# An attention, gate and feed-forward kernel on one core: low-half matmuls moved to the end of each sum, and a new order of pieces

## The chip, the cores and the metric

The kernel runs on one core of one Trainium2 chip. The metric is the device time of one execution in microseconds (us), the median of several. The core has five engines that run side by side and wait for each other through semaphores: PE (TensorE, matmul; its weight loads are PEld), ACT (ScalarE), DVE (VectorE), POOL (GpSimd) and SP (SyncE), which issues nearly all transfers.

## The reference

```python
def reference(q, k, v, moe_*, moe2_*):              # cut to what matters
    a = softmax(concat(q k^T / 8 inside a band of +-15 keys, q kmax^T / 8 + log 32))   # kmax: max over 32 keys
    x = a @ concat(v, mean of v over 32 keys)       # (2, 8, 768, 64) -> (2, 768, 512)
    gate = sigmoid(5-tap causal convolution of x)
    g = gate * (x @ w_val)                          # then @ w_out
    h = relu(g @ w_out @ w_in)                      # 512 -> 1024, halves u and v
    s = w_spatial @ layernorm(v) + b_spatial        # 768 x 768 over the sequence
    return (u * s) @ w_out2                         # (2, 768, 512)
```

Some weights arrive as 64-bit floats.

## The kernel before, in words

Every large product is computed to nearly fp32 accuracy from two halves of each operand: a high half (the value cast to a shorter float) and a low half (the rest). A product over a contraction is three matmuls for each chunk of 128: high by high, high by low, low by high. ACT casts the high halves, POOL (sometimes DVE) subtracts to get the low halves, so the low half is always the later one. The helper `mm3` writes these three matmuls next to each other, chunk after chunk.

The program is recorded as pieces, each of some instructions on several engines. Names that the text uses, with an index: `lk`, `lq`, `lv` load k, q and v of a pair of heads (8 pairs, 4 to a batch); `kw` builds the key windows; `score`, `at`, `pv` are scores with softmax, transposes and the product with v for one tick (16 ticks: a pair and a half of the sequence); `put` copies the means of v (`vm`, from `vsum`) into v's tile by a transfer; `gate` is the tanh; `val` is x @ w_val (16 pieces of 12 matmuls of 384 columns); `wp` is w_out @ w_in (8 pieces, the first four being one sweep over four banks; each ends with a matmul by `minus` that takes the scaled high half back out of the bank, and so waits for ACT's scaling); `v` and `u` are the halves of h (12 pieces of 512 columns, 16 of 384); `ws` and `wt` prepare w_spatial; `s` is the product over the sequence (8 plain pieces for the first batch, 14 for the second, which is computed with fewer products); `r` is the result (12 pieces). PSUM has 8 tiles (`psum()`, one bank each), handed out in rotation; `unit()` hands out 28 SBUF buffers in the same way.

`ORDER` is a text of piece names. The position of a piece there is the priority of its instructions. A list scheduler (`Planner.plan`) with a cost for every instruction then decides, engine by engine, which ready instruction goes next, and the program is written out in that order. Engines run their own list strictly in order. An edit of ORDER, or of the order of matmuls inside a piece, therefore shifts instructions on all engines. Every record in the profile carries line 195, where the scheduler issues, so groups are told apart by tiles.

Of the kernel before, what the change touches and what calls it, by code (L numbers as in the profile page):

```python
# [16 lines left out]
P = 128  # L17
# [22 lines left out]
LOOK = {"PE": 0, "ACT": 0, "DVE": 0, "POOL": 100, "SP": 200}  # L40

ORDER = """
    mask*2 wout in1*4 wout cw wp*2 wout masks wout in0*3 lk lq wp*2 lq kw lk kw in0 lv vsum lk*2 score put lq kw score
    wp at wp kw wval vsum score lq score lv*2 pv wp at score at put pv score at score wp lv wval*3 put*2 pv lq pv gate
    val*4 lk*2 ws at*2 score lv kw lv kw score pv*2 v u lq score u*3 at pv at pv gate val*2 vsum val vsum val u*3 put
    v ws*2 v*2 lk v*2 at*2 lq score ws*2 score kw pv*2 u lv ws score*2 lk kw s*4 at lq score*2 s at put*2 s at*2 pv*3
    lv pv at put pv s*2 wt at pv gate val*3 gate val*2 out2 val*3 v*3 out2 v out2 v*2 u*3 wt*2 u s*2 u*3 s out2 u s*5
    r*6 s*2 r*3 s*4 r*3
"""

WIN = 10240 / 3
# [286 lines left out]
def tile_kernel(ctx, tc, q, k, v, vn, w_val, conv_w, w_out, w_in, w_sp, b_sp, w_out2, mask_l, mask_r, eye, out):  # L338
# [328 lines left out]
    def val(i):  # L667
        (b, g), m = divmod(i // KT, NC), i % KT
        need("gate", i // KT + 1)
        need("wval", KT)  # L670
        po = psum()[:, :CH]
        for e in range(KT):
            w = W["val", e, 0]
            mm3(po, [t[:, m * P : (m + 1) * P] for t in w], [X[b, g, e][:, a] for a in (0, 1)], e == 0, e == KT - 1)
        z = Z[b, g][:, m]
        dve.scalar_tensor_tensor(z, z, 1.0, po, op0=ALU.add, op1=ALU.mult)
        gg = G[b, g, m] = gh.get().rearrange("p (a s) -> p a s", a=2)
        copy("ghi", gg[:, 0], z)
        sub("glo", gg[:, 1], z, f(gg[:, 0]))
# [3 lines left out]
    def vhalf(i):  # L683
# [3 lines left out]
        need("wp", KT)  # L687
        po = psum()
        ts_ = slice(t * P - g * CH, (t + 1) * P - g * CH)
        for e in range(KT):  # L690
            mm3(po, [G[b, g, e][:, a, ts_] for a in (0, 1)], W["p", e, 1], e == 0, e == KT - 1)
        if b < B - 1:
            h = hs.get()
        elif t < NT // 2:
# [75 lines left out]
    def fast_s(i):  # L770
# [8 lines left out]
        if first:  # L779
            BANK[key] = psum()[:, :CH]  # L780
        po = BANK[key]
        for t in range(n):
# [9 lines left out]
            for k, (a, c) in enumerate(((0, 0), (0, 1), (1, 0))):  # L792
                pe.matmul(po, A[a], Bs[c], start=first and t == 0 and k == 0, stop=t == n - 1 and k == 2, skip_group_check=True)
# [16 lines left out]
    def uhalf(i):  # L810
        (b, g), m = divmod(i // KT, NC), i % KT
        need("val", KT * (i // KT + 1))
        need("wp", 2 * KT)
        if g == 0:
            U[b, m] = uu.get()
        po = psum()[:, :CH]
        for e in range(KT):
            w = W["p", e, 0]
            mm3(po, [t[:, m * P : (m + 1) * P] for t in w], [G[b, g, e][:, a] for a in (0, 1)], e == 0, e == KT - 1)
# [17 lines left out]
    def spatial(i):  # L837
        if i >= (B - 1) * NC * KT:
            return fast_s(i - (B - 1) * NC * KT)
        (b, g), m = divmod(i // KT, NC), i % KT  # L840
        cs = slice(g * CH, (g + 1) * CH)
        need("v", NT * (b + 1))
        need("u", KT * (i // KT + 1))
        need("ws", NT)
        po = psum()[:, :CH]
        for t in range(NT):
            mm3(po, [w[:, m * P : (m + 1) * P] for w in VN[b, t]], [WS[t][:, a, cs] for a in (0, 1)], t == 0, t == NT - 1)
        finish_s(b, g, m, po, bias[:, cs], str(i))

    os_ = Parts(512, F32)  # L850
# [1 line left out]
    def result(i):  # L852
# [7 lines left out]
        for c in range(parts):  # L860
            cs = slice(c * DM // parts, (c + 1) * DM // parts)
            po = psum()[:, cs]
            for e in range(KT):
                mm3(po, [Y[b, g, e][:, a, ts_] for a in (0, 1)], [w[:, cs] for w in W["out2", e, 0]], e == 0, e == KT - 1)
            act.copy(o[:, cs], po)
            sp.dma_start(out[b, t * P : (t + 1) * P, cs], o[:, cs])

# [14 lines left out]
    def w_product():  # L882
# [17 lines left out]
        for n in (1, 0):  # L900
# [141 lines left out]
```

## Time and profile before

| | |
|---|---|
| median of 3 runs | 287.33 us (287.33 to 287.96) |
| the profiled execution: its own time | 286.44 us |
| its span, first to last instruction | 284.7 us |
| PE busy | 259.7 us, 91% of the span |
| DVE, ACT, POOL busy | 190.0, 166.2, 149.3 us |

Busy time of PE is the time in which at least one matmul is on its way; a matmul's record is longer than the step from one matmul to the next, because they overlap. The time of the profiled execution is 1.7 us more than its span.

### The profile page before, as it was taken

Reading aid. Unit: us, or ns where it says so; the run is one execution under the profiler, and the core shown is the slowest. Engines: PE = TensorE matmul, PEld = TensorE weight load, DVE = VectorE, ACT = ScalarE, POOL = GpSimd, SP = SyncE. Lnnn points to the kernel's source line nnn. Section 1 sums busy time; section 2 is a strip of 40 time slices with the busy share of each in tenths; the row PEclk is TensorE's granted clock in tenths of the full one; section 3 lists DMA queues with packets and bytes.
Section 4 is the critical chain, followed back from the end, with each engine's and each line's share of the span. In section 5 each row is a group of like instructions: output and inputs, shape, how many; then the busy total and the mean of one; then the engine's idle time right before and its main releaser. Section 6 shows DMA issues by size and latency. Waiting matters only on the chain.

```text
span 284.7 us, 5456 instructions
## 1 busy us (share of the span) xinstructions
PE 259.7 (91%) x1958; PEld 228.7 (80%) x1958; DVE 190.0 (67%) x426; ACT 166.2 (58%) x446; POOL 149.3 (52%) x172
## 2 busy tenths in 40 slices
PE   0599987898999999999899997999998999999995
PEld 0367655668889898989889997997898988988985
DVE  2795867698698797465986678973863895741250
ACT  4698965998895835559557891456234561332322
POOL 7689553227764338557544650369556288522050
PEclk9999999999999999999999999999999999999999
DMA  7999995899381144300040007012020330105203
GB/s 197 377 404 273 316 220 137 240 251 336 86 222 59 58 117 146 113 0 3 0 105 1 2 17 198 2 60 89 0 76 1 111 113 0 74 29 194 111 0 111
DMA packets 14330, 34.51 MB, mean 121 GB/s; under 512 B 1949, under 2 KB 4544, under 8 KB 14304
## 3 DMA queue, kind: packets, MB, share of 16 engines
q1 hardware_dynamic: 14112, 34.02, 39.7%
q8 instruction: 15, 0.25, 0.4%
q0 software_dynamic: 192, 0.15, 0.2%
q14 instruction: 11, 0.09, 0.1%
HBM read 29.84 MB, written 3.15 MB: 116 GB/s over the span
## 4 chain that ended last, share of the span: by engine, by line
PE 53%; DMA 21%; ACT 9%; DVE 7%; POOL 5%; issue 2%; SPq 1%; POOLq 0%; DVEq 0%; ACTq 0%
PE ps L195 53%; DMA u<-in_moe_w_in_dram 6%; ACT a L195 5%; DMA u<-in_v_dram 5%; DVE u L195 4%; POOL u L195 4%; ACT u L195 4%; DMA u<-in_moe_w_val_dram 4%; DMA u<-in_moe_w_spatial_dram 3%; DMA u<-vm 3%; SPq L195 1%; DVE ps L195 1%; DVE a L195 1%; POOL a L195 1%; ACT aT L195 0%
## 5 line engine op out<-in xcount | busy, mean ns | idle before, releaser
L195 PE MATMUL ps<-u,u 128*128 128x384 f32 (+3 forms) x1434 | 229.8, 346 | 16.1 <-ACT u L195 12.2
L195 PEld LDWEIGHTS ps<-u,u 128*128 128x128 f32 (+1 forms) x1434 | 201.3, 200 | 38.3 <-ACT u L195 14.0
L195 POOL TENSOR_TENSOR u<-u,u 128x384 fp32r<-128x384 f32 (+3 forms) x76 | 102.5, 1364 | 90.5 <-ACT u L195 80.0
L195 ACT CAST u<-u 128x384 fp32r<-128x384 f32 (+3 forms) x76 | 45.8, 636 | 46.0 <-DVE u L195 34.4
L195 POOL TENSOR_TENSOR a<-a,sm 128x360 f32<-128x360 f32 x32 | 26.3, 844 | 28.4 <-DVE sm L195 17.2
L195 DVE SCALAR_TENSOR_TENSOR u<-ps,cw,u 128x384 f32<-128x384 f32 (+3 forms) x64 | 37.0, 607 | 0.0
L195 ACT ACTIVATE u<-ps 128x512 fp32r<-128x512 f32 (+2 forms) x44 | 23.5, 565 | 20.7 <-PE ps L195 16.6
L195 ACT ACTIVATE a<-ps,nm 128x120 f32<-128x120 f32 x48 | 17.0, 363 | 5.5 <-DVE nm L195 4.5
L195 ACT ACTIVATE a<-a,nm 128x120 f32<-128x120 f32 x48 | 18.5, 394 | 2.8 <-DVE nm L195 1.7
L195 DVE BATCH_NORM_STATS2 st<-u 128x6 f32<-128x512 f32 x12 | 8.3, 693 | 16.4 <-ACT u L195 16.4
L195 DVE TENSOR_SCALAR u<-u 128x512 uint32<-128x512 uint32 (+1 forms) x21 | 13.0, 627 | 7.6 <-DMA u<-in_moe_w_out_dram 5.3
L195 DVE TENSOR_TENSOR u<-u 128x384 f32<-128x384 f32 (+5 forms) x28 | 17.9, 650 | 0.2
L195 ACT ACTIVATE ps<-u 128x512 f32<-128x512 f32 x20 | 12.8, 647 | 6.0 <-DMA u<-in_moe_w_in_dram 3.1
L195 DVE SCALAR_TENSOR_TENSOR u<-ps,u 128x512 uint32<-128x512 uint32 x20 | 13.7, 689 | 2.6 <-ACT ps L195 1.4
L195 PEld LDWEIGHTS ps<-aT,u 120*64 120x64 f32 x384 | 12.5, 137 | 3.5 <-issue 1.7
L195 PE MATMUL ps<-aT,u 120*64 120x64 f32 x384 | 13.8, 225 | 1.6 <-DMA u<-in_v_dram 1.4
L195 ACT COPY aT<-ps 120x384 f32<-120x384 f32 x32 | 13.9, 494 | 1.9 <-PE ps L195 1.8
L195 ACT COPY u<-ps 128x512 f32<-128x512 f32 (+1 forms) x13 | 6.8, 562 | 13.6 <-PE ps L195 13.6
L195 DVE TENSOR_TENSOR u<-ps,u 128x384 fp32r<-128x384 f32 (+1 forms) x20 | 10.9, 552 | 5.0 <-ACT u L195 4.0
L195 DVE TENSOR_SCALAR sm<-ps 128x3 f32<-128x3 f32 x32 | 5.1, 159 | 13.7 <-ACT a L195 13.3
L195 DVE TENSOR_TENSOR u<-u,u 128x384 f32<-128x384 f32 (+2 forms) x16 | 14.0, 889 | 0.1
L195 DVE TENSOR_TENSOR gatef<-ps,u 128x384 f32<-128x384 f32 x6 | 3.3, 557 | 15.2 <-PE ps L195 15.2
(54 smaller groups left out, 197.4 us busy)
## 6 DMA issues: line engine op xcount, KB each, us to landing
u<-in_moe_w_spatial_dram SPq DMA_DIRECT2D x12, 384.0 KB, 3.3
u<-in_moe_w_out_dram SPq DMA_DIRECT2D x8, 512.0 KB, 10.4
u<-in_moe_w_in_dram SPq DMA_DIRECT2D x8, 512.0 KB
ks<-in_k_dram SPq DMA_DIRECT2D x8, 384.0 KB, 8.1
u<-in_q_dram SPq DMA_DIRECT2D x8, 384.0 KB, 9.3
u<-in_v_dram SPq DMA_DIRECT2D x16, 192.0 KB, 9.0
u<-in_vn_dram SPq DMA_DIRECT2D x8, 384.0 KB, 7.5
out_dram<-u SPq DMA_DIRECT2D x11, 256.0 KB, 2.8
```

Source lines behind the costliest of these rows:

```text
L195: getattr(real, method)(*args, **kw)
```

## The change: order inside the sums, and a new ORDER

A new helper `product` takes the list of operand pairs of one sum and writes the matmuls in another order: first, for each chunk, high by high and the product with the low half that is ready early; then, for all chunks, the product with the low half of the operand that comes late. `late` says which of the two operands that is. `val`, `v`, `u`, `s` (both batches) and `r` use it. In the first sweep of `wp` the three kinds go one after the other over the four banks. ORDER is replaced; so the scheduler's lists change on every engine. The numbers of instructions of each kind on each engine are the same in both programs.

```diff
+    def product(o, pairs, late, first=True, **kw):
+        todo = [(a[0], b[0]) for a, b in pairs], [(a[0], b[1]) for a, b in pairs], [(a[1], b[0]) for a, b in pairs]
+        todo = [x for y in zip(todo[0], todo[1] if late == 0 else todo[2]) for x in y] + (todo[2] if late == 0 else todo[1])
+        for i, (a, b) in enumerate(todo):
+            pe.matmul(o, a, b, start=first and i == 0, stop=i == len(todo) - 1, **kw)
...
-        for e in range(KT):
-            mm3(po, [G[b, g, e][:, a, ts_] for a in (0, 1)], W["p", e, 1], e == 0, e == KT - 1)
+        product(po, [([G[b, g, e][:, a, ts_] for a in (0, 1)], W["p", e, 1]) for e in range(KT)], 0)
...
-                for e in range(KT):
-                    mm3(pos[e], [t[:, e * P : (e + 1) * P] for t in W["ot", i, 0]], W["in", i, n], i == 0, i == KT - 1)
+                for k, (a, b) in enumerate(((0, 0), (0, 1), (1, 0))):
+                    for e in range(KT):
+                        pe.matmul(pos[e], W["ot", i, 0][a][:, e * P : (e + 1) * P], W["in", i, n][b], start=i == 0 and k == 0, stop=i == KT - 1 and k == 2)
...
-    mask*2 wout in1*4 wout cw wp*2 wout masks wout in0*3 lk lq wp*2 lq kw lk kw in0 lv vsum lk*2 score put lq kw score
+    wout in1 mask wout mask wp in1 wp in1 wout wp cw in1 wout wval in0*4 wp lk wp kw lq lk kw masks score lq score lq
```

**First place: PE, the first sweep of wp.** Before, at the end of the first chunk (`ps_104` is the fourth bank; `mrow`, `mcol` and `edge` are the attention mask, two tiles of which are built here):

```order
L195 MATMUL ps_103<-u_88,u_85 128x512 x2
L195 MATMUL ps_104<-u_88,u_85 128x512 x3
L195 LDWEIGHTS mcol
L195 MATMUL ps_107<-mrow,mcol 128x360
L195 LDWEIGHTS mcol
L195 MATMUL ps_107<-edge,mcol 64x16
```

Now, at the same place (`ps_92` to `ps_95` are the four banks, `u_98` holds the second chunk of w_in, `u_91` the second of w_out):

```order
L195 MATMUL ps_93<-u_88,u_85 128x512
L195 MATMUL ps_94<-u_88,u_85 128x512
L195 MATMUL ps_95<-u_88,u_85 128x512
L195 MATMUL ps_92<-u_98,u_85 128x512
L195 MATMUL ps_93<-u_98,u_85 128x512
L195 MATMUL ps_94<-u_98,u_85 128x512
L195 MATMUL ps_95<-u_98,u_85 128x512
```

The second chunk now follows the first at once, and the four mask matmuls moved behind all 48 matmuls of the sweep.

**Second place: ACT, the scaling of wp4 and wp5.** Before (`a_148`, `a_149` are the exponentials of tick 1, `ps_150` and `ps_156` the sums of wp4 and wp5, `a_169` tick 2):

```order
L195 ACTIVATE a_149,ps_145<-ps_145,nm_146 128x120
L195 ACTIVATE u_123<-ps_150 128x512
L195 COPY u_157<-ks_78 128x12x64
L195 COPY aT_153<-ps_152 120x384
L195 ACTIVATE u_151<-ps_150 128x512
L195 COPY aT_155<-ps_154 120x384
L195 ACTIVATE ps_160<-u_159 128x512
L195 ACTIVATE u_151<-ps_156 128x512 x2
```

Now (`ps_127` is wp4, `a_140` and `a_141` tick 0, `a_146` and `a_147` tick 1, `ps_158` wp5):

```order
L195 ACTIVATE u_128<-ps_127 128x512
L195 CAST u_112<-u_149 128x512
L195 ACTIVATE a_140,ps_136<-ps_136,nm_138 128x120 x3
L195 ACTIVATE a_141,ps_137<-ps_137,nm_138 128x120 x3
L195 ACTIVATE a_146,ps_142<-ps_142,nm_144 128x120 x3
L195 ACTIVATE a_147,ps_143<-ps_143,nm_144 128x120 x3
L195 ACTIVATE u_128<-ps_158 128x512 x2
L195 ACTIVATE a_166,ps_162<-ps_162,nm_164 128x120 x3
```

The scaling of wp4 moved ahead of the exponentials of ticks 0 and 1, that of wp5 behind all twelve of them.

**Third place: POOL, the clearing of v's last tile** (after which SP may issue the loads of the last pair; `u_442` before, `u_389` now). Before, with the softmax scaling of tick 15 (`a_416`, `a_417`) ahead of it:

```order
L195 TENSOR_TENSOR u_419<-u_278,u_419 128x384
L195 TENSOR_TENSOR a_416<-a_416,sm_415 128x360
L195 TENSOR_TENSOR a_417<-a_417,sm_415 128x360
L195 TENSOR_TENSOR u_419<-u_278,u_419 128x384
L195 MEMSET u_442 32x2x64 x2
```

Now, with tick 13 (`a_376`, `a_377`) ahead of it and tick 14 (`a_409`) behind:

```order
L195 TENSOR_TENSOR a_376<-a_376,sm_375 128x360
L195 TENSOR_TENSOR u_365<-u_348,u_352 128x512
L195 TENSOR_TENSOR a_377<-a_377,sm_375 128x360
L195 MEMSET u_389 32x2x64 x2
L195 TENSOR_TENSOR va_396<-va_396,power 128x1
L195 TENSOR_TENSOR u_386<-u_385,u_386 128x768
L195 TENSOR_TENSOR u_390<-u_385,u_390 128x768
L195 TENSOR_TENSOR a_409<-a_409,sm_408 128x360
```

The clearing now stands two ticks earlier, ahead of the last two low halves of w_spatial (`u_386`, `u_390`).

## Rows read from the trace of the kernel before

**Rows 1.** Page, part 1: busy time and share of the span, instructions.

```profile
span 284.7 us, 5456 instructions
PE 259.7 (91%) x1958; PEld 228.7 (80%) x1958; DVE 190.0 (67%) x426; ACT 166.2 (58%) x446; POOL 149.3 (52%) x172
```

**Rows 2.** Busy time by stretch, with granted clock, DMA share and GB/s.

```profile
core 0: us, PE busy (x) PEld busy (x) DVE busy (x) ACT busy (x) POOL busy (x), PEclk, DMA share, GB/s
0.00:20.00 20.00, 9.35 (x28) 6.32 (x29) 12.69 (x19) 12.67 (x23) 14.16 (x29) 1.00 0.91 321
20.00:40.00 20.00, 18.44 (x130) 13.32 (x128) 14.65 (x29) 18.00 (x49) 15.38 (x23) 1.00 1.04 287
40.00:60.00 20.00, 16.42 (x210) 12.41 (x211) 14.04 (x36) 14.47 (x57) 5.09 (x8) 1.00 0.83 196
60.00:80.00 20.00, 18.68 (x220) 16.57 (x218) 16.31 (x38) 17.36 (x51) 13.86 (x20) 1.00 0.80 228
80.00:110.00 30.00, 29.55 (x224) 27.09 (x219) 25.60 (x63) 21.07 (x66) 12.43 (x14) 1.00 0.43 125
110.00:200.00 90.00, 86.65 (x745) 80.05 (x744) 62.49 (x157) 54.29 (x156) 51.26 (x56) 1.00 0.16 48
```

**Rows 3.** Groups by form, PE: busy, mean ns of one, idle before.

```profile
L195 PE MATMUL ps<-u,u 128*128 128x384 f32 x654 | 120.5, 338 | 2.1 <-ACT u L195 1.3 <-POOL u L195 0.6 <-ACT aT L195 0.2
L195 PE MATMUL ps<-u,u 128*128 128x512 f32 x372 | 93.7, 403 | 11.6 <-ACT u L195 10.9 <-POOL u L195 0.4 <-ACT aT L195 0.3
```

**Rows 4.** Timeline, PE, 0 to 26 us: start, length, what, idle before.

```profile
10.34 5.81 PE L195 MATMUL ps<-u,u 128*128 128x512 f32 x12 [10.34 <-ACT u L195]
15.95 0.52 PE L195 MATMUL ps<-mrow,mcol 67*128 67x360 bf16 x1
...
16.83 0.20 PE L195 MATMUL ps<-edge,mcol 67*64 67x16 bf16 x1
17.34 8.46 PE L195 MATMUL ps<-u,u 128*128 128x512 f32 x36 [0.31 <-ACT u L195]
```

**Rows 5.** Timeline, PE, 186 to 192 us.

```profile
185.81 5.36 PE L195 MATMUL ps<-u,u 128*128 128x384 f32 x30
191.45 4.91 PE L195 MATMUL ps<-u,u 128*128 128x512 f32 x19 [0.27 <-ACT u L195]
```

**Rows 6.** What PE waited for, 20 to 110 us: total, times, longest.

```profile
PE ps L195 <- ACT u L195: 4.0, 5, 1.4
PE ps L195 <- DMA u<-in_q_dram: 1.6, 1, 1.6
```

**Rows 7.** Timeline, PE, 36 to 67 us, around its waits, and 78 us.

```profile
36.36 0.50 PE L195 MATMUL ps<-u,minus 128*128 128x512 f32 x1 [0.52 <-ACT u L195]
...
40.11 0.50 PE L195 MATMUL ps<-u,minus 128*128 128x512 f32 x1 [0.77 <-ACT u L195]
...
51.95 0.51 PE L195 MATMUL ps<-u,minus 128*128 128x512 f32 x1 [1.40 <-ACT u L195]
...
66.56 0.50 PE L195 MATMUL ps<-u,minus 128*128 128x512 f32 x1 [0.85 <-ACT u L195]
...
78.58 1.62 PE L195 MATMUL ps<-aT,u 120*64 120x64 f32 x48
```

**Rows 8.** Timeline, ACT, 42 to 50 us and 76 to 79 us.

```profile
42.88 0.36 ACT L195 ACTIVATE a<-ps,nm 128x120 f32<-128x120 f32 x1 [1.43 <-DVE nm L195]
...
43.33 0.36 ACT L195 ACTIVATE a<-ps,nm 128x120 f32<-128x120 f32 x1
...
48.67 0.36 ACT L195 ACTIVATE a<-ps,nm 128x120 f32<-128x120 f32 x1 [2.87 <-DVE nm L195]
...
76.82 0.85 ACT L195 COPY aT<-ps 120x384 f32<-120x384 f32 x2
```

**Rows 9.** Groups by form, ACT.

```profile
L195 ACT CAST u<-u 128x384 fp32r<-128x384 f32 x32 | 14.8, 512 | 14.0 <-DVE u L195 7.9 <-POOL u L195 4.8 <-PE ps L195 1.3
L195 ACT CAST u<-u 128x768 fp32r<-128x768 f32 x12 | 10.0, 836 | 14.7 <-DVE u L195 11.1 <-DMA u<-in_moe_w_spatial_dram 2.1 <-POOL u L195 1.4
L195 ACT COPY u<-ks 128x768 f32<-128x768 f32 x8 | 6.6, 841 | 3.1 <-POOL u L195 3.1
```

**Rows 10.** Timeline, PE, 126 to 221 us, around its waits.

```profile
126.11 1.89 PE L195 MATMUL ps<-u,u 64*64 64x120 f32 x48
127.93 1.62 PE L195 MATMUL ps<-aT,u 120*64 120x64 f32 x48
...
137.65 5.53 PE L195 MATMUL ps<-u,u 64*64 64x120 f32 x66 [0.79 <-POOL u L195]
143.77 2.55 PE L195 MATMUL ps<-u,u 128*128 128x384 f32 x13 [0.60 <-POOL u L195]
...
169.53 0.82 PE L195 MATMUL ps<-ident,a 128*120 128x128 f32 x6
170.59 3.24 PE L195 MATMUL ps<-u,u 128*128 128x384 f32 x17 [0.24 <-ACT aT L195]
175.27 1.99 PE L195 MATMUL ps<-aT,u 120*64 120x64 f32 x48 [1.44 <-DMA u<-in_v_dram]
...
220.68 3.59 PE L195 MATMUL ps<-u,u 128*128 128x384 f32 x19 [0.84 <-ACT u L195]
```

**Rows 11.** Chain that ended last, 168 to 221 us: start, length, what.

```profile
168.29 0.20 POOL u L195
...
171.11 4.02 DMA u<-in_v_dram
...
175.27 1.87 PE ps L195 x46
...
215.72 1.28 ACT u L195
...
217.07 2.95 POOL u L195
...
220.03 0.61 ACT u L195
...
220.68 3.42 PE ps L195 x18
```

More of the change, by code (lines that the diff above doesn't have):

```diff
@@ L42 @@
 ORDER = """
-    mask*2 wout in1*4 wout cw wp*2 wout masks wout in0*3 lk lq wp*2 lq kw lk kw in0 lv vsum lk*2 score put lq kw score
[L44 to L48, printed above, removed]
+    wout in1 mask wout mask wp in1 wp in1 wout wp cw in1 wout wval in0*4 wp lk wp kw lq lk kw masks score lq score lq
+    wval lk vsum lv lk kw wp vsum score lk lq put wp kw score lv put score at pv wval lv at pv lk wp score put wval at
+    pv lv put ws*3 at score pv vsum gate val*3 kw val score at*2 pv*2 v u*2 vsum at lq at pv kw pv gate u score*2 val
+    u ws lv lk kw lk kw val*3 lq score*2 v lq put lv put v at v at*2 v score*2 pv lv pv ws u*2 lv ws u*2 v at*2 put lq
+    score*2 out2 pv*3 s*4 at*2 s*2 at pv put pv*2 s*2 gate val*3 gate val*2 out2 val*3 out2 v out2 v u v*4 u*3 wt*3 r
+    s*3 u s u*3 s*2 r*3 s*6 r*2 s r*2 s r*4
 """
@@ L671, in val @@
         po = psum()[:, :CH]
-        for e in range(KT):
-            w = W["val", e, 0]
-            mm3(po, [t[:, m * P : (m + 1) * P] for t in w], [X[b, g, e][:, a] for a in (0, 1)], e == 0, e == KT - 1)
+        product(po, [([t[:, m * P : (m + 1) * P] for t in W["val", e, 0]], [X[b, g, e][:, a] for a in (0, 1)]) for e in range(KT)], 1)
         z = Z[b, g][:, m]
@@ L781, in fast_s @@
         po = BANK[key]
+        pairs = []
         for t in range(n):
@@ L791, in fast_s @@
                 Bs = [y[:, k_ * CH : (k_ + 1) * CH] for y in FT[t]]
-            for k, (a, c) in enumerate(((0, 0), (0, 1), (1, 0))):
-                pe.matmul(po, A[a], Bs[c], start=first and t == 0 and k == 0, stop=t == n - 1 and k == 2, skip_group_check=True)
+            pairs.append((A, Bs))
+        product(po, pairs, 0, first, skip_group_check=True)
         if x == 1:
@@ L816, in uhalf @@
         po = psum()[:, :CH]
-        for e in range(KT):
-            w = W["p", e, 0]
-            mm3(po, [t[:, m * P : (m + 1) * P] for t in w], [G[b, g, e][:, a] for a in (0, 1)], e == 0, e == KT - 1)
+        product(po, [([t[:, m * P : (m + 1) * P] for t in W["p", e, 0]], [G[b, g, e][:, a] for a in (0, 1)]) for e in range(KT)], 1)
         o = U[b, m][:, g * CH : (g + 1) * CH]
@@ L845, in spatial @@
         po = psum()[:, :CH]
-        for t in range(NT):
-            mm3(po, [w[:, m * P : (m + 1) * P] for w in VN[b, t]], [WS[t][:, a, cs] for a in (0, 1)], t == 0, t == NT - 1)
+        product(po, [([w[:, m * P : (m + 1) * P] for w in VN[b, t]], [WS[t][:, a, cs] for a in (0, 1)]) for t in range(NT)], 0)
         finish_s(b, g, m, po, bias[:, cs], str(i))
@@ L862, in result @@
             po = psum()[:, cs]
-            for e in range(KT):
-                mm3(po, [Y[b, g, e][:, a, ts_] for a in (0, 1)], [w[:, cs] for w in W["out2", e, 0]], e == 0, e == KT - 1)
+            product(po, [([Y[b, g, e][:, a, ts_] for a in (0, 1)], [w[:, cs] for w in W["out2", e, 0]]) for e in range(KT)], 0)
             act.copy(o[:, cs], po)
@@ L914, in w_product @@
                 need(f"in{n}", i + 1)
-                for e in range(KT):
-                    mm3(pos[e], [t[:, e * P : (e + 1) * P] for t in W["ot", i, 0]], W["in", i, n], i == 0, i == KT - 1)
+                for k, (a, b) in enumerate(((0, 0), (0, 1), (1, 0))):
+                    for e in range(KT):
+                        pe.matmul(pos[e], W["ot", i, 0][a][:, e * P : (e + 1) * P], W["in", i, n][b], start=i == 0 and k == 0, stop=i == KT - 1 and k == 2)
                 if i == KT - 1:
```

## The prediction

> **What bounds the kernel now.** I began with the busy times and then asked where the busiest engine stands still. PE is busy for 259.7 of 284.7 us, DVE for 190.0, ACT for 166.2 [rows 1]: the kernel is bound by PE, and 25.0 us of the span are without a matmul. Neither program has a matmul more or less than the other, so the change can move only PE's standstill, and its slow start. The reader is to look at two things: the steps of a dense stretch, and the places between.
>
> In a dense stretch thirty matmuls of 384 columns take 5.36 us [rows 5]; less one record of 0.338 us [rows 3] that is 5.02 over 29 steps, 0.173 us a step. For 512 columns 36 take 8.46 us [rows 4]; less a record of 0.403 [rows 3], 8.06 over 35 steps is 0.230. These hold whatever follows whatever: a weight load goes with every matmul (1958 of each [rows 1]), also where two matmuls in a row use the same weights. Writing high by high, low by high in turn therefore costs nothing by itself. Since a record is 0.165 us longer than a step, a stop costs some 0.165 us more than the idle time that a row names.
>
> The stretches say where the stops are [rows 2]. PE's idle time is 10.65 us up to 20 us (10.34 of it ahead of the first matmul [rows 4]), then 1.56, 3.58 and 1.32 in three stretches of 20, then 0.45, and 3.35 in the 90 us from 110 on. From 20 to 80 us ACT is the next engine, busy 49.83 of 60, with DMA at 0.80 to 1.04 and the loads far behind their issue. The list of waits gives the names [rows 6]: five waits of PE for ACT, 4.0 us, one of 1.6 for q. Four of the five are the matmul by `minus` at the end of a wp piece [rows 7]: PE stands behind ACT's scaling of that bank. After 110 us the waits are single and of several kinds [rows 10].
>
> **The change part by part.** I sum against the profiled execution (span 284.7 us, its own time 286.44) and apply the difference to the median 287.33; its time is 0.89 below the median, which is the error of that step.
>
> *A, the sweep of wp.* The first load, its casts and so the first matmul are in the same order on SP, DVE and ACT, so the start stays at 10.34. Before, twelve matmuls go at (5.81 - 0.40)/11 = 0.49 us a step, four mask matmuls follow, PE stops for 0.31, and 36 go at 0.230 until 25.80 [rows 4]. The first pace is about that of the lower of the clock's two levels, 1.2 GHz, the second of 2.4; the row of granted clock says 1.00 for the whole stretch and does not resolve it [rows 2]. Somewhere between 15.95 and 17.34 the pace changed; I take 16.7. Now 13 matmuls fit before that, and 35 at 0.230 plus the end of a record bring 24.9, so -0.9. The w_out chunk that is needed last is the eighth load in both orders. The masks come back later at the fast pace: 1.08 us of slow records [rows 4], half of it, +0.5. A is -0.4, between -0.9 and 0.
>
> *B, from the sweep to the transposes of tick 5.* This is ACT's stretch. The transposes' copies end at 77.7 [rows 8] and pv4 starts at 78.58 [rows 7]. Up to the same copies ACT now has four casts of 384 columns (the high halves of val0 to val3) and two of 768 (ws1, ws2) more, and one copy of 768 less: 4 x 0.512 + 2 x 0.836 - 0.841 = 2.9 us [rows 9]. Against it: PE's wait of 1.6 for q goes, because tick 3 is placed later, and with it some of the 2.87 us in which ACT stood ahead of tick 3's exponentials [rows 8]; I take the smaller, since q of pair 3 is issued later too. And PE has more behind it at pv4: seven matmuls of v0 (7 x 0.230 = 1.6) less one tick of scores, half of 1.89 [rows 10], so 0.65. B is 2.9 - 1.6 - 0.65 = +0.65. Its bounds are far apart. If all six waits of PE go, -(4.0 + 1.6 + 6 x 0.165) = -6.6; if ACT gives nothing back and the waits at wp grow, some +4.5 (the rival below). I stay by the sum of ACT's own work, since ACT has only 10 us to spare in these 60. The work is not wasted: ws1, ws2 are then done, but PE is dense from 80 to 110 anyway, so nothing is taken back there, and I count 0.
>
> *C, 110 us to the products of the second batch.* Five waits stand here: 0.79, 0.60, 0.24, 1.44 [rows 10] and 0.27 [rows 5], 3.34 us, with 5 x 0.165 some 4.2. The 1.44 us is the load of v for the last pair: POOL clears its tile at 168.29, SP issues after that, the transfer lands at 175.13 (171.11 + 4.02) [rows 11]. The clearing now stands on POOL two ticks earlier, ahead of the last w_spatial halves, and pv14 comes behind s5 rather than inside val9; this wait goes. The 0.79 and 0.60 are POOL's: the key windows of tick 12 and the low half of the last w_spatial tile. The windows are built some twenty POOL operations earlier now, and the low halves of v and w_spatial end each sum, as `product` does it, with 26 matmuls of s0 to s2 (4.5 us) ahead of the first use of the last tile. The 0.24 and 0.27 lie in tick 15's wake and go with it. What is late next: v5's high half. ACT casts it behind ten exponentials of ticks 14 and 15, 0.455 us a step [rows 8], 4.6 us, on top of two ticks' copies, two w_spatial casts and three pv's. PE has meanwhile two pairs of transposes (1.6), two ticks of scores (1.9), three pv's (2.4) [rows 10] and those 4.5, 10.4 us. That is about even; I put 0.5 there and 0.7 for what I do not see. C is -4.2 + 1.2 = -3.0, between -4.2 and 0.
>
> *D, the end.* One wait, 0.84 at 220.68 [rows 10]. The chain runs from PE through an ACT cast of 1.28, a POOL subtraction of 2.95 and an ACT operation of 0.61 back to PE [rows 11]: the slow low halves of v hold a buffer, ACT cannot write the next relu, and PE finds no bank. Now u12 is scaled ahead of u10 and u11, and r0 to r2 and six s sums are open meanwhile, so I leave the wait in: 0, between -1.0 and +1.0. The result pieces at the very end are the same 24 matmuls.
>
> The sum is -0.4 + 0.65 - 3.0 + 0 = -2.75: span 282.0, median 284.6.
>
> **The rivals.** *Slower, by ACT at wp5 to wp7.* Between the scalings of wp4 and wp5 ACT now has all twelve exponentials of ticks 0 and 1, 12 x 0.455 = 5.5 us, and these begin some 1.4 us behind PE's scores. PE's own work up to wp5's `minus` matmul is the rest of two ticks (1.2), nine matmuls of wp5 (2.1), tick 2 (0.95 and its masks) and two of wp6 (0.5), about 5.0. So PE stands for 2.5 us where it stood for 0.77 [rows 7], and wp6 and wp7 stand behind six more exponentials and behind two ticks and two pv's in the same way, 1 us each beyond what they were. With ACT's 2.9 not recovered B becomes +4.5, and the time 287.33 - 0.4 + 4.5 - 3.0 = 288.4. For it: four of the five waits for ACT are of just this kind. Against it: wp4 is scaled earlier, wp7 has two ticks of other work around it. It decides from B = +4.3.
>
> *No change.* The work after 110 us could run into banks. Three pv sums (pv10 to pv12) now wait on DVE behind the reading of s0 to s2, so seven sums are open when the transposes of tick 13 ask for two banks. Two convolutions of four steps and their sums cost 3 us there, which makes C 0 and the time 287.6. The trace speaks for such a mechanism with the 0.84 us of D, against it with nothing of the kind between 80 and 200 us. The Trainium skill (PSUM — Partial Sum Buffer, Specifications) gives eight banks per partition, and a sum that is kept open for its late half holds one of them longer: by that rule alone the change lengthens every hold and the time would not fall; the trace agrees only at 220.68, with 0.84 us.
>
> *Faster by more.* The waits for ACT and q before 80 us go as well: B about -3.5, time 280.4. For it: ACT idles 5.5 us from 40 to 60 [rows 2]. Against it: ACT's 2.9 us more.
>
> That the reordered sums do nothing because the low halves were ready anyway is likely for most sums; it would leave ORDER's effect, most of C, standing.
>
> **How the numbers follow.** The forecast with its own range of 283.0 to 285.8: 0.48; faster by more: 0.14; a small gain between: 0.05; no change: 0.16; slower: 0.17. A difference of 0.3%, 0.9 us, is about what a measurement of this kernel can tell from none. So faster is 0.67, same 0.16, slower 0.17. From 280.7 to 288.2 holds all but some 0.06 below and 0.13 above.
>
> **What would show it.** A: the 48 matmuls of the sweep without a stop, ending near 24.9. B: pv4 starting at about 79, and waits of PE for ACT between 20 and 80 of 3 to 5 us. If one of them at wp5 exceeds 2.5, the slower rival is at work. C: no wait for v after 110 us and PE idle there under 1.5 us where it was 3.35. D: a wait of about 0.8 near u12. The prediction is wrong if pv4 starts after 82, if the transfers issued ahead of put0 land late enough to hold pv0, or if a wait of over 2 us shows at s0 or at the transposes of tick 13.

## The result, and the profile after

After: 279.28 us (median of 4 executions, 279.03 to 281.12), before beside it 287.33 (4 executions, 286.47 to 287.96); the ratio is 0.974, 95% interval 0.969 to 0.979. The forecast was 284.6, with a range from 280.7 to 288.2: the kernel became faster by 8 us and not by 2.75, and ended below the range. Medians, here and below, are of all executions of a kernel; the ratios leave out those over 1.5% above the kernel's fastest.

Part 1 of the page of after, as [rows 1]:

```profile
span 277.3 us, 5457 instructions
PE 259.3 (94%) x1958; PEld 229.0 (83%) x1958; DVE 191.1 (69%) x426; ACT 166.2 (60%) x446; POOL 150.8 (54%) x172
```

PE's busy time fell by 0.4 us, its standstill from 25.0 to 18.0. So the frame of the prediction held: only standstill and slow matmuls could go. The stretches of after, as [rows 2], with the last one added:

```profile
core 0: us, PE busy (x) PEld busy (x) DVE busy (x) ACT busy (x) POOL busy (x), PEclk, DMA share, GB/s
0.00:20.00 20.00, 11.04 (x38) 8.33 (x39) 13.04 (x21) 13.11 (x22) 14.87 (x30) 1.00 0.93 342
20.00:40.00 20.00, 16.72 (x131) 11.13 (x129) 14.32 (x30) 17.83 (x50) 13.92 (x19) 1.00 1.04 298
40.00:60.00 20.00, 18.78 (x205) 14.25 (x205) 13.78 (x38) 17.14 (x61) 9.11 (x14) 0.91 0.78 195
60.00:80.00 20.00, 19.76 (x207) 16.87 (x204) 17.20 (x38) 18.06 (x59) 14.32 (x13) 1.00 0.93 254
80.00:110.00 30.00, 29.87 (x282) 27.65 (x280) 25.78 (x65) 22.30 (x71) 14.75 (x22) 1.00 0.25 70
110.00:200.00 90.00, 88.98 (x722) 83.17 (x721) 65.93 (x167) 52.55 (x149) 49.61 (x56) 1.00 0.19 56
200.00:278.00 78.00, 74.14 (x386) 67.57 (x384) 41.05 (x72) 25.20 (x42) 34.22 (x22) 0.99 0.20 71
```

Up to 20 us PE has 38 matmuls behind it where it had 28, and there is a new thing: a granted clock of 0.91 from 40 to 60. The sweep of wp in PE's timeline, as [rows 4], with the stops behind it:

```profile
8.81 13.96 PE L195 MATMUL ps<-u,u 128*128 128x512 f32 x49 [8.81 <-ACT u L195]
22.62 0.33 PE L195 MATMUL ps<-mrow,mcol 67*128 67x360 bf16 x1
...
23.61 0.99 PE L195 MATMUL ps<-u,minus 128*128 128x512 f32 x2 [0.54 <-ACT u L195]
```

The sweep starts 1.53 us earlier and runs without a stop that the timeline names (one gap, ahead of its fifth matmul, is 0.14 us). The row's 49 matmuls, the last of them wp4's, end at 22.77, so the sweep itself ends at 22.55 where it ended at 25.80. What PE waited for, first from 20 to 110 us, as [rows 6], then from 110 us to the end:

```profile
PE ps L195 <- ACT u L195: 3.4, 4, 1.8
PE ps L195 <- DVE u L195: 1.3, 1, 1.3
```

```profile
PE ps L195 <- ACT aT L195: 0.6, 1, 0.6
PE ps L195 <- DVE nm L195: 0.3, 1, 0.3
```

The waits for v and at u12 [rows 10] are gone, and so is the one for q [rows 6]; the one for DVE, 1.3 us ahead of tick 0's scores, is new.

To compare programs with different orders I take, from PE's records, three points at which PE has done the same work in both, to one or two matmuls: the end of val7, the end of val15 and the end of the last matmul. Before: 104.8, 191.2, 281.5. After: 101.6, 185.9, 274.1. So 3.2 us were gained up to val7, 2.1 from there to val15 and 2.1 behind it, together 7.4, which is the difference of the spans.

### The profile page after: what moved, and what is told of

Its sections match the earlier page's. It is cut to its first block, busy times and chain, and to the rows that moved or that the text cites. A ratio compares the mean times of both kernels' runs of the same rounds, so it can differ in the third digit from the quotient of the medians.

```text
span 277.3 us, 5457 instructions
## 1 busy us (share of the span) xinstructions
PE 259.3 (94%) x1958; PEld 229.0 (83%) x1958; DVE 191.1 (69%) x426; ACT 166.2 (60%) x446; POOL 150.8 (54%) x172
## 4 chain that ended last, share of the span: by engine, by line
PE 57%; DVE 15%; ACT 13%; DMA 9%; issue 4%; SPq 1%; DVEq 0%; ACTq 0%
PE ps L195 57%; DVE u L195 9%; ACT a L195 9%; DMA ks<-in_k_dram 4%; DMA u<-in_moe_w_out_dram 3%; ACT u L195 3%; DVE ps L195 2%; DMA u<-in_moe_w_spatial_dram 2%; DVE a L195 1%; DVE st L195 1%; DVE km L195 1%; SPq L195 1%; ACT aT L195 1%; DVE nm L195 0%; DVE va L195 0%
## 5 line engine op out<-in xcount | busy, mean ns | idle before, releaser
L195 PEld LDWEIGHTS ps<-u,u 128*128 128x128 f32 (+1 forms) x1434 | 201.8, 201 | 32.3 <-ACT u L195 10.2
L195 POOL TENSOR_TENSOR u<-u,u 128x384 fp32r<-128x384 f32 (+3 forms) x76 | 102.9, 1369 | 66.9 <-ACT u L195 65.2
L195 ACT CAST u<-u 128x384 fp32r<-128x384 f32 (+3 forms) x76 | 46.5, 636 | 46.9 <-DVE u L195 24.1
L195 POOL TENSOR_TENSOR va<-va,power 128x1 f32<-128x1 f32 x12 | 7.3, 610 | 21.6 <-DVE va L195 21.5
L195 DVE TENSOR_TENSOR u<-u,u 128x256 f32<-128x256 f32 (+2 forms) x16 | 17.1, 1069 | 0.8 <-DMA u<-in_moe_w_spatial_dram 0.6
L195 DVE TENSOR_TENSOR u<-u 128x256 f32<-128x256 f32 (+5 forms) x28 | 13.8, 497 | 0.3
```

The costliest lines, as they stand in the source:

```text
L195: getattr(real, method)(*args, **kw)
```

## The experiments

The table holds all of them, with before and after; the times of before beside them were 287.0 to 288.0. "First" is the start of the first matmul; the other columns are the three stretches between the points above, in the profiled execution.

| kernel | median us | ratio to before, 95% | first | to val7 | val7 to val15 | val15 to end |
|---|---|---|---|---|---|---|
| before | 287.33 | 1 | 10.34 | 104.8 | 86.4 | 90.3 |
| after | 279.28 | 0.974 (0.969 to 0.979) | 8.81 | 101.6 | 84.3 | 88.2 |
| e1 sums and sweep, old ORDER | 304.10 | 1.054 (1.044 to 1.064) | 10.44 | 104.4 | 93.0 | 100.7 |
| e2 new ORDER alone | 281.83 | 0.980 (0.976 to 0.984) | 8.96 | 105.8 | 82.8 | 88.2 |
| e3 before, loads alternate | 282.51 | 0.982 (0.978 to 0.986) | 8.79 | 101.3 | 85.9 | 90.3 |
| e4 after, loads put back | 287.44 | 0.999 (0.997 to 1.001) | 10.43 | 112.1 | 82.5 | 88.3 |
| l, third load w_out | 284.84 | 0.990 (0.986 to 0.993) | 8.81 | 101.8 | 86.2 | 90.3 |
| l, third load w_val | 287.29 | 0.998 (0.996 to 1.001) | 8.82 | 106.7 | 86.1 | 90.2 |
| g1 sweep alone, old ORDER | 285.82 | 0.994 (0.991 to 0.997) | 10.68 | 107.5 | 85.8 | 90.3 |
| g2 sums alone, old ORDER | 302.13 | 1.048 (1.044 to 1.051) | 10.65 | 106.0 | 93.2 | 97.7 |
| p, after with the old sweep | 281.35 | 0.979 (0.975 to 0.982) | 9.02 | 104.8 | 82.5 | 88.3 |
| p, after with the old sums | 278.86 | 0.970 (0.967 to 0.973) | 8.86 | 104.4 | 82.4 | 88.1 |
| c, v cleared earlier | 289.42 | 1.007 (1.004 to 1.010) | 10.00 | 106.6 | 87.4 | 89.4 |
| d, tail of ORDER alone | 301.29 | 1.047 (1.043 to 1.051) | 10.61 | 105.8 | 85.9 | 103.2 |
| d2, u8 ahead of v8 | 288.77 | 1.003 (1.000 to 1.006) | 10.30 | 106.8 | 85.9 | 91.8 |
| c1, wp5 ahead of tick 1 | 282.63 | 0.982 (0.979 to 0.985) | 9.15 | 106.4 | 82.5 | 89.2 |
| c3, wp5 ahead of ticks 0, 1 | 288.03 | 1.002 (0.999 to 1.005) | 9.15 | 111.2 | 82.6 | 89.2 |
| f1, PE's stop filled | 281.06 | 0.977 (0.973 to 0.981) | 8.69 | 102.9 | 84.4 | 89.5 |
| h1, e3 and g1 together | 283.53 | 0.984 (0.978 to 0.991) | 9.03 | 101.3 | 85.8 | 90.3 |
| h2, h1 and ORDER behind val7 | 282.83 | 0.983 (0.978 to 0.988) | 8.68 | 105.2 | 85.3 | 88.1 |

**The two halves of the change.** e1 is before with the new sums and the new sweep; e2 is after with both as they were.

> The new order inside the sums (and in the sweep of wp) with the old ORDER. Theory P (it is the new ORDER that pays, since most low halves were ready anyway): the median stays within 1.5 us of the kernel before, 286 to 288; the first matmul stays at 10.3 us, since the loads go in the old order; PE's waits for POOL after 110 us (0.79 and 0.60 before) shrink. Theory S (the sums pay: they let PE start work that waited for low halves): 283 or less, with fewer stops between 110 and 200 us.

> The new ORDER with the old order inside the sums. Theory P: 280 to 282, first matmul at 8.8 us as in the changed kernel. Theory S: 284 or more, with stops at matmuls that wait for POOL's low halves; the first matmul still at 8.8.

The sums and the sweep do not work by themselves: beside the old ORDER they cost 16 us. ORDER alone gives most of the gain, 6.1 of 8 us. Both stretches behind val7 are as short with ORDER alone (82.8, 88.2) as in after (84.3, 88.2).

**The first loads.** e3 changes only the first line of before's ORDER, e4 only that of after, where the four chunks of w_in stand in a row again:

```diff
e3
-    mask*2 wout in1*4 wout cw wp*2 wout masks wout in0*3
+    mask*2 wout in1 wout in1*2 wout in1 wout cw wp*2 masks in0*3
e4
-    wout in1 mask wout mask wp in1 wp in1 wout wp cw in1 wout wval
+    wout in1*4 mask wout mask wp*2 wout wp cw wout wval
```

> The kernel before with one edit in ORDER: the first eight loads alternate between w_out and w_in instead of four of w_in in a row (the mask tiles' place is the same, ahead of the last part of the sweep). Theory L (the place of the third load sets PE's start, since ACT's cast of the first w_in chunk stands behind the third load's first step): first matmul at 8.8 instead of 10.3 us, clock up some 1.5 to 3 us earlier, sweep's 48 matmuls done near 23 instead of 25.8, and the whole kernel 1 to 3 us faster, as far as the stops behind it do not take it back. Rival N (the early landing was a chance of that execution): first matmul at 10.3 +- 0.3, time as before within 1 us.

> The changed kernel with one edit in ORDER: all four loads of w_in ahead of the second of w_out, as before. Theory L: first matmul back at 10.3 us, clock up later, sweep done near 25, the kernel 1.5 to 3 us slower than the changed one (281 to 282.5). Rival N: first matmul at 8.8 or anywhere, time of the changed kernel (279.3 +- 0.8).

Both went further than expected: e3 gains 5.4 us, e4 loses all 8. The cause of the start stands in ACT's timeline. Before, up to the first matmul at 10.34 (ACTIVATE is the first step of splitting a loaded chunk, CAST the last on ACT):

```profile
6.61 0.63 ACT L195 ACTIVATE ps<-u 128x512 f32<-128x512 f32 x1 [0.57 <-DMA u<-in_moe_w_in_dram]
9.10 0.66 ACT L195 ACTIVATE ps<-u 128x512 f32<-128x512 f32 x1 [1.85 <-DMA u<-in_moe_w_in_dram]
9.67 0.62 ACT L195 CAST u<-u 128x512 fp32r<-128x512 f32 x1
```

After:

```profile
6.10 0.65 ACT L195 ACTIVATE ps<-u 128x512 f32<-128x512 f32 x1
7.57 0.66 ACT L195 ACTIVATE ps<-u 128x512 f32<-128x512 f32 x1 [0.81 <-DMA u<-in_moe_w_out_dram]
8.14 0.62 ACT L195 CAST u<-u 128x512 fp32r<-128x512 f32 x1
```

The cast that the first matmul needs, of the second load, stands on ACT behind the first step for the third load. In before that is a second chunk of w_in, whose step starts at 9.10, in after a second of w_out, at 7.57; both steps start when the chunk has landed. To see what in the order counts, the next two change the third load alone: "wout in1 wout in1*3" and "wout in1 wval in1*3" for "wout in1*4".

> Before, with the second chunk of w_out loaded third instead of sixth (the three w_in chunks behind it keep their order). Theory T (the third load decides when ACT gets to the cast that the first matmul needs; a second chunk of w_out lands sooner than a second of w_in): first matmul at 8.8 to 9.1 instead of 10.3, time 283 to 286 beside 287.3. Rival Q (all loads must alternate): first matmul at 10 or later, time within 1 us of before.

> Before, with the first chunk of w_val loaded third, ahead of the second chunk of w_in. Theory T (the third load is late where it reads the same tensor as the second): first matmul at 8.8 to 9.1 as with w_out third; the sweep's second chunk comes one load later, so the time is 284 to 288. Rival O (only the number of loads ahead counts, or w_out's place): first matmul at 10 or later, 288 to 290.

The chunk of w_val lands at 7.57 too:

```profile
7.57 0.66 ACT L195 ACTIVATE ps<-u 128x512 f32<-128x512 f32 x1 [0.98 <-DMA u<-in_moe_w_val_dram]
8.14 0.62 ACT L195 CAST u<-u 128x512 fp32r<-128x512 f32 x1
...
17.49 9.85 PE L195 MATMUL ps<-u,u 128*128 128x512 f32 x35 [1.63 <-ACT u L195]
```

Over all kernels the first matmul starts at 8.68 to 9.15 in the twelve whose third load is of w_out or w_val, and at 10.00 to 10.68 in the eight in which it is of w_in. The last of the three rows says why the early start alone is worth nothing: with w_val third, the sweep runs out of chunks, PE stands 1.63 us ahead of the second one, and before's time is back. With w_out third 2.6 us are gained, with both tensors nearly in turn 5.4.

The start is thus only a part of what the order of the loads is worth. In e3 the wait for q is gone as well, and PE waits for ACT for 2.1 us from 20 to 110 us instead of 4.0. In e4 the sweep, too, runs out of chunks:

```profile
10.43 4.86 PE L195 MATMUL ps<-u,u 128*128 128x512 f32 x12 [10.43 <-ACT u L195]
17.27 10.04 PE L195 MATMUL ps<-u,u 128*128 128x512 f32 x36 [1.98 <-ACT u L195]
```

It ends at 27.31, 4.8 us later than in after. From there to pv4 e4 takes 59.9 us and after 54.3. PE's idle time in that stretch differs by only 0.6 us (5.3 and 4.7), but e4 has 13.6 us at half clock there, from 58.8 to 62.2 and from 65.6 to 75.8, and after 3.4: the rest of the difference is slow matmuls.

**Sums and sweep apart.** "p" is after with one of the two put back, g1 and g2 are before with one of the two.

> After's ORDER and its sums of val, v, u, s and r, with the old order of matmuls in the first sweep of wp. With both orders old the time was 281.8, with both new 279.3. Theory S (the sweep's order makes the 2.5 us, by when the clock rises and what ACT does first): 281 to 282.5. Theory P (the product sums make it): 278.5 to 280.

> After's ORDER and its new sweep of wp, with the old order of matmuls in the sums of val, v, u, s and r. Theory S: 278.5 to 280. Theory P: 281 to 282.5. If neither half alone gives 2.5 us, what decides is whether a half-clock spell falls into the stretch up to pv5.

> Before, with the new order of matmuls in the first sweep of wp alone (its sums and ORDER). With after's ORDER this edit saved some 2.5 us. Theory S (a sweep that is served high by high first is better wherever it stands): 284.5 to 286 beside 287.3. Theory O (it only fits the new ORDER; here the loads come late and the masks stand inside the sweep): 286.5 to 290.

> Before, with the new order inside the sums of val, v, u, s and r alone (its sweep and ORDER). Sums and sweep together gave 304.1, with stops of 4.1 us inside s0 and 2.8 at pv15. Theory N (each sum now asks for the operand that counts as early three or more steps sooner, and in the old ORDER it is not there yet): 298 to 304, with the stop at s0 above 3 us. Rival W (the 16 us are the sweep's, by half-clock spells behind it): 286 to 290.

The sweep is the half that gains: 0.970 with it against 0.980 without in the new ORDER (p with old sums against e2; the intervals are apart), and 0.994 in the old one. The sums of `product` gain nothing in the new ORDER (0.974 with, 0.970 without, intervals that overlap) and make the whole loss in the old one. Where, PE's timeline of g2 shows at s0:

```profile
131.23 3.29 PE L195 MATMUL ps<-u,u 128*128 128x384 f32 x18
138.45 2.93 PE L195 MATMUL ps<-u,u 128*128 128x384 f32 x8 [3.93 <-DVE u L195]
```

s0 stops after eight matmuls, high by high and high by low of four chunks, because the ninth needs the high half of v4. ACT's timeline of g2 has the cast of that half at 137.78:

```profile
137.78 0.62 ACT L195 CAST u<-u 128x512 fp32r<-128x512 f32 x1
```

In before the same cast stands at 127.39, together with v3's, ahead of s0's first matmul at 131.67. So it is not four matmuls' difference within the sum (the ninth instead of the thirteenth, 0.7 us). ORDER is the same in both, but the planner lays the engines' lists by its own estimates, and with the new sums it puts the last steps of v4's statistics and its normalising on DVE, 132.65 to 137.26 us, behind most of the softmax of ticks 10 and 11; in before they end at 126.88, ahead of it. Why its estimates tip over there was not tried. This stop is 3.93 of g2's 14 us. Others stand at pv15 (2.58), at s9 (2.77) and from 241 to 249 us (0.49, 1.46 and 0.74), and behind the stops at s0 and s9 matmuls of 384 columns go at 0.32 us a step instead of 0.173; these were not followed to their causes. Beside the new ORDER v4's cast is at 130.92, ahead of s0 at 138.55, and nothing waits.

**Term C: the wait for v.** c moves one token of before's ORDER, the last lv, so that POOL clears v's last tile ahead of s4, the scaling of tick 15 and s5:

```diff
-    s at put*2 s at*2 pv*3 lv pv at put pv s*2
+    s at put*2 lv s at*2 pv*4 at put pv s*2
```

> Before, with the lv token of the last pair alone six tokens earlier in ORDER, so that POOL clears v's last tile ahead of s4, the scaling of tick 15 and s5 instead of behind them; SP can issue its load earlier. pv14 and val8 move up on PE with it. Theory V (the 1.6 us stop at pv14 is only this clearing): the stop goes, val7 to val15 takes 84.5 to 85.0 instead of 86.4, time 286.0 to 286.6 beside 287.9. Rival N (PE then stands for what is next in line, the transposes of tick 15 or val8's operand): 86 or more in that stretch and under 0.6 us gained.

PE's timeline of c at the same place as the 1.44 us of before [rows 10]:

```profile
170.49 1.21 PE L195 MATMUL ps<-aT,u 120*64 120x64 f32 x24 [0.58 <-POOL u L195]
...
175.17 0.79 PE L195 MATMUL ps<-u,u 128*128 128x384 f32 x3 [1.05 <-DVE u L195]
176.77 0.92 PE L195 MATMUL ps<-aT,u 120*64 120x64 f32 x24 [0.81 <-DVE u L195]
```

The wait for v is gone, 1.44 us, and three others stand there, 2.44 (one of them was 0.24 before). The stretch is 1.0 longer. The rival of this experiment holds: the load was only the last of several things that came late there.

**Term D: the wait at u12.** d takes before with after's tokens from the last val pieces on. d2 moves one u token ahead of the third v token, so that ACT empties u8's and u9's banks ahead of v10's:

```diff
d
-    out2 val*3 v*3 out2 v out2 v*2 u*3 wt*2 u s*2 u*3 s out2 u s*5 r*6 s*2 r*3 s*4 r*3
+    out2 val*3 out2 v out2 v u v*4 u*3 wt*2 r s*3 u s u*3 s*2 r*3 s*6 r*2 s r*2 s r*4
d2
-    val*3 v*3 out2 v out2 v*2 u*3 wt*2
+    val*3 v*2 u v out2 v out2 v*2 u*2 wt*2
```

> Before, with after's order of tokens from the last val pieces to the end alone (the same counts of pieces; sums as before). Before has PE stops of 0.44 us at v6 and 1.0 us at u12 there, and 90.3 us from the end of val15 to the end of r11; after has neither stop and 88.2. Theory T (the order of these last pieces is what term D missed): 88.0 to 88.7 in that stretch, time 285.5 to 286.5 beside 287.9. Rival R (the stops go because of what stands earlier, such as the second tick's windows or the w_spatial halves): 90 or more in that stretch, time 287.3 to 288.5.

> Before, with one u token moved ahead of the third v token of the second batch, so that ACT empties u8's bank ahead of v8's and u9's ahead of those of v10 and v11, as in after. Theory B (PE's stop of 1.0 us at u12 is for one of these banks): that stop goes, val15 to the end of r11 takes 88.8 to 89.4 instead of 90.3, time 286 to 286.6 beside 287.3. Rival P (POOL's low halves of v, 2.95 us each, set the pace, and the stop moves to s8 or s10): 90 or more in that stretch, time 287 to 288.

d is far off both theories: the tail without what goes ahead of it costs 14 us, with a stop of 3.66 us at u14 and three more for s10, of 0.83 to 1.89 us. It shows that the tail does not stand for itself, and says nothing on the wait. d2 is cleaner:

```profile
217.81 21.06 PE L195 MATMUL ps<-u,u 128*128 128x384 f32 x110
...
244.16 2.01 PE L195 MATMUL ps<-u,u 128*128 128x384 f32 x10 [1.17 <-ACT u L195]
```

PE runs through u12, as meant, and stands 1.17 us for ACT 25 us later. The rival holds: the chain that ended last runs there through 4.28 us of POOL and 0.84 of ACT to that matmul, and the bank was only where it showed.

**ACT at wp5, and the clock.** After has a stop of 1.82 us at wp5's matmul by `minus`, and a half clock behind it:

```profile
40.42 0.57 PE L195 MATMUL ps<-u,minus 128*128 128x512 f32 x1 [1.82 <-ACT u L195]
```

These are the stretches around it (the row of 3.40 us has the granted clock 0.50):

```profile
36.00:40.70 4.70, 2.88 (x33) 1.74 (x33) 3.89 (x14) 4.18 (x21) 1.58 (x2) 1.00 1.03 267
40.70:44.10 3.40, 3.40 (x9) 2.65 (x9) 1.35 (x5) 2.92 (x13) 1.56 (x2) 0.50 1.07 264
44.10:48.00 3.90, 3.89 (x42) 2.55 (x42) 2.90 (x5) 2.12 (x5) 3.00 (x5) 1.00 0.47 125
```

wp6's matmuls stand 0.43 us apart there instead of 0.23. c1 and c3 move wp5 ahead in after's ORDER ("score lq wp score" and "wp score lq score" for "score lq score ... wp"); f1 leaves the order and fills PE's stop with work:

```diff
         for o in self.plan():
             real, method, args, kw = o.call
+            if fill and o.eng == "PE" and o.piece == ("wp", 6):
+                for i in range(fill):
+                    getattr(real, method)(*args, **dict(kw, stop=True))
+                fill = 0
             getattr(real, method)(*args, **kw)
```

> After, with wp5 one token earlier in ORDER, so that ACT scales wp5's bank between the exponentials of tick 0 and tick 1 instead of behind both. In after PE stands 1.98 us at 38.2 for this scaling and the granted clock is 0.5 from 40.7 to 44.1. Theory K (that stop brings the clock down): both go, some 2.0 us of stop and half of 3.4 us of slow matmuls, 1.7, less up to 1.5 that comes back as a wait for tick 1's exponentials: 275.5 to 277.5, no half-clock rows ahead of the last microseconds. Theory W (ACT is the bound there, the wait only moves): the stop shows again ahead of the transposes of tick 0 or 1, val7 ends at 101 to 102 as in after, time 278.5 to 280.

> After, with wp5 two tokens earlier, so that ACT scales wp5's bank ahead of the exponentials of ticks 0 and 1. Theory K: no stop of 1.98 us at 38 and no half clock behind it, 275.5 to 277.5. Theory W: ACT must wait for wp5's sum before any exponential, and a stop of 1.5 to 3 us shows at wp6, at the scores of tick 2 or at the transposes of tick 0; 279 to 282.

> After, with PE kept at work in the 1.98 us in which it stands ahead of wp5's last matmul: the first matmul of wp6, which stands just ahead of the stop, is issued nine times instead of once (each of the extra eight is a sum of its own that the ninth overwrites; the output stays that of after). 8 x 0.227 = 1.8 us. Nothing else moves. Theory K (the stop brings the clock down): no granted clock of 0.5 at 40.7 to 44.1, wp6's matmuls 0.23 us apart instead of 0.43, and 1.5 to 2 us less, 277.0 to 278.0. Rival A (the clock falls for another reason, or ACT sets the pace there anyway): the spell stays, or it goes and PE waits for ACT behind it; 279 to 279.8.

c1 and c3 are slower than after: ACT's work moves, and PE stands for ACT and DVE elsewhere (c3 up to 2.9 us at wp6). In f1 the stop is gone, and wp6 runs at the full clock:

```profile
40.21 2.14 PE L198 MATMUL ps<-u,u 128*128 128x512 f32 x8
42.19 0.62 PE L200 MATMUL ps<-u,u 128*128 128x512 f32 x2
42.78 0.50 PE L200 MATMUL ps<-u,minus 128*128 128x512 f32 x1
43.12 2.45 PE L200 MATMUL ps<-u,u 128*128 128x512 f32 x10
```

But f1 is not faster. Its profiled execution has another half clock, 28.0 to 34.9 us, behind the stop at score0 that after has too. Three of its six executions show a mean clock of 1.000, no half clock anywhere, and took 279.31, 280.05 and 280.33 us; after's four, at 0.992 to 0.994, took 279.03 to 281.12. So that theory falls: filling the stop takes its half clock away, and no time is gained by it. PE then stands for ACT 0.63 us at wp6, where after has no stop, and 0.80 us at wp7, as in after (0.79).

**Do the stages add?** h1 is e3 with g1's sweep, h2 adds after's tokens behind val7, still with the old sums.

> Before with its first eight loads alternating (282.5 alone) and the new order of matmuls in the first sweep of wp (285.8 alone beside 288.0); old sums, old order of pieces. Theory A (the two add): val7 ends at 98 to 100 and the time is 279.5 to 281. Theory M (with the loads in time the sweep has nothing left to gain): val7 at 101 to 102, 282 to 283.5. Behind val7 the stops of before at s1, s2, pv14, v6 and u12 are all still there, 176 us from val7 to the end of r11.

> h1 with after's order of tokens behind val7; still the old sums. Theory Z (the order of pieces behind val7 makes C and D, whatever stands ahead): 172.3 to 173 us from val7 to the end of r11 as in after, 3.5 to 4.2 us under h1, so 276 to 279. Rival G (the order behind val7 needs the v, u and w_spatial work that after has done ahead of it): new stops of 2 us and more at s0 or at the transposes of tick 13, at or above h1.

With the loads in time the sweep has nothing left to gain in the old order (0.984 against e3's 0.982). In h2 the last stretch is after's, 88.1 instead of 90.3, though the old order stood ahead of val7, but from val7 to val15 it takes 85.3 and not 82.4, with new waits:

```profile
142.14 0.91 PE L195 MATMUL ps<-aT,u 120*64 120x64 f32 x22 [1.28 <-ACT aT L195]
...
150.45 1.84 PE L195 MATMUL ps<-u,u 128*128 128x384 f32 x9 [0.76 <-ACT u L195]
```

That order leans on work that after has done before val7. No experiment beats after by more than the measurement can tell.

## Why the prediction was wrong

Set against the prediction's own steps, in the profiled executions, the 7.4 us come so:

| step | booked | measured |
|---|---|---|
| to the sweep's end (A without the masks) | -0.9 | -3.25 (25.80 to 22.55) |
| from there to pv4 (B without its 0.65, and A's masks) | +1.8 | +1.6 (52.8 us to 54.3) |
| pv4 to the end of val7 (B's 0.65) | -0.65 | -1.5 (26.2 to 24.7) |
| val7 to val15 (C without the wait at v6) | -2.6 | -2.1 |
| val15 to the end (C's wait at v6, and D) | -0.4 | -2.1 |

Two terms are set where their work stands: the 0.65 us of matmuls that are done ahead of pv4 shorten the stretch behind it, and the wait at v6 [rows 5], 0.27 us and 0.165 for the stop, which C took in, lies behind val15.

**A failed, and with it the most.** The step reads "The first load, its casts and so the first matmul are in the same order on SP, DVE and ACT, so the start stays at 10.34". It left out what stands between them on ACT: the first step for the third load, and the change replaces that load. The start moved to 8.81. For the start e3, e4 and the two l kernels show it; e3 and e4 show what the order of the loads is worth, 5.4 and 8 us, and the kernel with w_val third that the start alone is worth nothing.

The text also let the second chunk follow the first at once, as if it were there. In all eight kernels whose third load is of w_in the second chunk's 36 matmuls start at 17.04 to 17.56, whether the four masks stand ahead of them (17.34 in before) or not (17.27 in e4, behind a stop of 1.98 for ACT). There the second chunk of w_out, the sixth load in before, sets the sweep's end: its cast on ACT ends at 17.29 in before and at 17.22 in e4, and at 11.09 in after, where it is the third load. So the 0.9 us that was booked needed the new loads as well. The new order inside the sweep has the smaller part: with the early loads and the old sweep it ends at 23.20 (e2) and 23.65 (p), 0.7 to 1.1 us behind after's. The pace does not decide it: in g2, which starts at 10.65, the matmuls are fast from 14 us on, in before from 16.5, and both sweeps end within 0.1 us of each other.

One misreading was without effect: slow records are 0.6 us long and not 0.40, so most of the steps that the text has at 0.49 are 0.43.

The Trainium skill (TensorE: Matmul & The Clock Gate, the table of specifications at its head) says that ScalarE takes its instructions strictly in turn. By that rule the cast cannot pass the step ahead of it, and both traces agree: 9.67 behind 9.10, and 8.14 behind 7.57.

**B was right in after,** to 0.2 us. ACT sets that stretch: it is busy for 53.0 us from 20 to 80 where it was 49.8, 3.2 us more for the 2.9 that were booked; the waits for ACT are 3.4 us, where 3 to 5 were forecast, the one for q is gone, and the stretch became longer, as booked. pv4 starts at 76.9 and not at 79 only because the sweep ended earlier. But the text had nothing that ties B to the loads: in e4, with the start that A assumed, the same order of pieces makes the stretch 7.1 us longer than in before. That B came out so well is in part luck. The rival at wp5 did occur, with 1.82 us instead of 2.5, below its point of decision; c1, c3 and f1 show that no time hangs on that one place.

**From pv4 to val7 too little was booked.** "PE is dense there anyway, so nothing is taken back there" put at nothing the 0.45 us of standstill in that stretch [rows 2], all of which goes. One matmul of v, 0.23 us, is also done behind val7 instead of ahead of it.

**C had the right sign and four fifths of the size.** The view was right: no wait for v, PE idle for 1.02 us from 110 to 200 us. But "this wait goes" was told too simply: c shows that with the clearing alone it goes and 1 us more of others takes its place. What gains is the whole order of that stretch; in e2 it gains 3.6 us. In after the part from val7 to v5 takes 31.4 us, in p with the old sweep, which comes to val7 3.2 us later, 29.6: part of an early arrival is given back there.

**D failed.** "So I leave the wait in: 0." The waits at v6 and u12 are gone, with their stops some 1.4 us, of which C had booked 0.4. The stretch takes 88.1 to 88.3 us in six kernels with the new order there, and 89.2 to 89.5 in c1, c3 and f1, where PE stands for 0.77 to 1.05 us for ACT at s18. f1 has after's lists but for eight matmuls ahead of wp5's end, so up to 1 us of the gain hangs on how the engines happen to meet there. d2 shows that u8's place, the nearest single reason, does not make it, and d that the tail alone does not either. Which of the moves does stays open.

**The rivals.** Slower, by ACT: not so. No change, by banks at tick 13: no wait stands at those transposes; the longest behind 110 us, 0.63 us, stands at tick 13's scores, for ACT's copy of other transposes. No row shows the late half of a sum holding PE up there. The Trainium skill (PSUM — Partial Sum Buffer, Specifications) gives eight banks; that a longer hold must cost time by this rule does not show here, where 0.9 us of waits are left from 110 us on. Faster by more came nearest in time, but by way of B, not of the start. The remark that the sums may do nothing by themselves was right with the new ORDER; that with another ORDER they do harm, 14 us in g2, it could not show.

## What to carry to other kernels

An operand is as early as what stands ahead of its cast on the engine that casts it: when a change permutes loads, follow every load's first step through the queue, not the first load alone, and ask which load the second batch of work needs. Where a planner makes the engines' lists, an edit inside a sum is an edit of all lists: the same sums cost 14 us beside one ORDER and nothing beside another, so such an edit is timed with the order that it will run in. And a wait that a trace names is often the last of several that end together: taking its named cause away moves the wait, here in c, d2 and f1, three times of three.

## What was not expected of the hardware

**Landing of the third load.** ACT can start on a third chunk of 512 KB 1.5 us later when it is of w_in, like the second, than when it is of w_out or w_val (9.10 against 7.57); the first matmul starts later in all eight kernels of the one kind than in the twelve of the other. Two rows of transfer rates, 0 to 14 us in 40 slices of 0.35 us, of before and then with w_val third:

```profile
GB/s 0 0 0 0 0 234 281 374 433 421 386 374 246 117 152 105 146 257 164 275 213 246 333 378 414 364 328 366 370 338 386 421 375 410 421 398 456 375 386 433
```

```profile
GB/s 0 0 0 0 12 222 293 351 374 375 257 211 293 293 351 401 459 432 395 349 280 263 217 246 374 397 413 440 413 410 410 386 445 410 398 410 386 445 410 398
```

From 4.5 to 7.7 us (the 14th to the 22nd number) before has 105 to 275 GB/s and the other 263 to 459. A chunk of w_in is half of each of its 128 rows, one of w_out or w_val is whole rows; whether that makes it, or that two loads of one tensor follow each other, was not tried.

**What the half clock costs.** Over 84 executions of before, those with a mean granted clock of 0.992 or more took 286.88 us (median of 26), those at 0.981 to 0.988 took 287.37 (34), those at 0.976 and below 288.50 (24). This compares executions and does not show which is the cause. The profiled execution of before is one at 1.000. Most half clocks of these kernels lie between 40 and 75 us; e1, g2 and d have more behind their long stops. What one costs is not the same everywhere: f1 shows one whose removal gave nothing back, and in e4 10.2 us more of them than in after go with some 5 us, while PE's idle time is nearly the same.
